# Softplus for two thirds of batch 0, masks ahead of the first sum, and a new order of instructions in a recurrence-and-mixer kernel

## The chip, the cores and the metric

The kernel runs on one core of a Trainium2 chip. Its engines work side by side, each through its own list of instructions: TensorE (PE, with its weight loads as PEld) for matrix products, VectorE (DVE), ScalarE (ACT) and GpSimd (POOL) for work on elements, and SyncE (SP), which only issues transfers. DMA engines move data between memory and the core; here SP, ACT and POOL issue these transfers. The metric is the time of one execution on the device in microseconds (us); lower is better.

## The reference

A gated linear recurrence runs over 768 steps for 4 batches and 8 heads of width 48, and its output goes through a mixer of two two-layer networks, one across the tokens and one across the channels.

```python
f = 1.0 / (1.0 + np.exp(-f_logit))
for t in range(S):
    state = f[:, :, t, :, None] * state + np.einsum('bhd,bhe->bhde', k[:, :, t], v[:, :, t])
    y[:, :, t] = np.einsum('bhd,bhde->bhe', q[:, :, t], state)
...
h = np.maximum(xt @ w_tok1, 0.0) @ w_tok2
u = x + h.transpose(0, 2, 1)
h2 = np.maximum(u @ w_ch1, 0.0) @ w_ch2
return (u + h2).astype(np.float32)
```

The kernel works with the logarithm of the gates: -log f = log(1 + exp(-f_logit)), which is Softplus of -f_logit.

## The kernel before

**Stages.** The 768 steps of a batch are cut into six chunks of 128, taken in pairs P = 0, 1, 2; the two steps of a pair that share a row are folded by an addition. For each batch b and pair P the stages are these.

- `gates` (line 447) makes -log f in place in `f_sb` with two passes on ACT, Exp (line 450) and Ln (line 452).
- `sums_and_turns` (line 456) adds the two steps into `two` (line 460), makes running sums with a triangular matrix `tri` on PE (line 472, and the totals at line 479), takes `first` from them (line 492), and exponentials of the sums into `GG` on ACT (lines 495 and 512). It multiplies q and k by `GG` into `qk` (line 516), and turns `qk` around into `qT` and `kT` (lines 541 and 543, later batches by a transfer).
- `attention` (line 556) makes scores from `kT` and `qT` (line 574), masks them into `AmT` (lines 612 to 617; for some of batch 0, ACT copies and POOL multiplies), updates the state from k and v (lines 592 and 626), copies it to `state_bd` (line 637) and forms the output of the pair (lines 650 and 658), which lands in `x_nat` and `x_bf`.
- `mixer` (line 697) runs the two networks over a batch: lines 702 and 718 across tokens, 759 to turn the result, 777 and 796 across channels. Line 802 adds the last product to `x_nat`, and SP stores the rows (line 695). The very last block is cut in two pieces, 288 and 96 columns wide.

**Masks and constants.** POOL makes `tri_bf` from ones (line 393). From it DVE makes `tri`, `tri2`, `ident` and six pieces of `mask` in eleven small steps (lines 396 to 408). `steady` holds the ones that fill matmuls read.

**Loads.** f of pair P0 of batch 0 comes in two halves, one issued by SP and one by ACT (`load_half`, line 342). SP issues f of P1 and, once POOL has marked it, f of P2. POOL issues everything else in one line: k and q of P0, v of P0, then k, q, v of P1 and of P2, the weights, and the later batches.

**What sets the order.** All steps are first collected in a plan. Each gets engines it may run on, what it needs, and a modelled cost. `ORDER` is a list written out in the file: each number, divided by four, names a step, and the rest of the division says which of its engines takes it. `best` (line 171) walks the list, gives each step a start time by the model, chooses the PSUM bank, and emits all steps sorted by that start. `SLOTS` and `HELD` are modelled landing times of loads. Every engine thus runs a fixed sequence, and waits are the only thing decided on the chip.

**Fills.** Where the model sees PE idle by over 250 ns ahead of 25.5 us, `best` inserts fill matmuls (`idle`, line 835), whose results nobody reads.

## Time and profile before

| | |
|---|---|
| median of three runs | 168.1 us (167.59 to 172.11) |
| the profiled execution, whole time | 167.82 us |
| its span, first to last instruction | 166.1 us |
| granted clock of PE | 1.00 of full speed |
| transferred | 24.34 MB, 68183 packets |

In the profile, a row of the timeline gives the start in us, the duration in us (of the merged row, if several follow each other), the engine, the line of the kernel, the operation, what it writes and reads, and how many instructions are merged. In brackets stands how long the engine was idle before it, and what ended that; "issue" means that nothing the profile shows was waited for. Durations of PE rows are partly modelled. In the rows of the DMA view the last number is the time from the issue to the landing in us.

### The profile page before, as it was taken

The page shows a single profiled execution, that of the slowest core. Times are in us where ns is not written, and L with a number is a line of the kernel's source. Part 1 is how long each engine was busy: PE and PEld are TensorE (multiplying, and loading weights), DVE is VectorE, ACT ScalarE, POOL GpSimd, SP SyncE. Part 2 cuts the span into 40 slices and gives each one's busy share as a digit, 9 for nine tenths or more (in the row PEclk, how much of TensorE's full clock was granted, in tenths as well). Part 3 has the DMA queues.
Part 4 walks back from the last instruction along what each step waited for, and adds up shares of the span by engine and source line. Part 5 has one row for each costly group of instructions (what it writes and reads, how often), then busy time and mean ns, then how long its engine had stood idle before and what let it go on. Part 6 is the DMA issues. An engine that isn't in the chain of part 4 may idle for free.

```text
span 166.1 us, 5049 instructions
## 1 busy us (share of the span) xinstructions
PE 158.2 (95%) x2086; PEld 103.8 (62%) x2086; DVE 129.3 (78%) x286; ACT 107.4 (65%) x228; POOL 63.6 (38%) x87
## 2 busy tenths in 40 slices
PE   5899969999999999999999999999999999999991
PEld 4587856566657775665656666656667665656660
DVE  6469994789999999999969989997897366915331
ACT  3788985899899999797799598375622522141200
POOL 7977589915877640020346623212122021000000
PEclk9999999999999999999999999999999999999999
DMA  5999999999999999698194999478310014900452
GB/s 131 218 176 173 201 211 240 188 233 208 211 222 218 249 226 248 76 92 213 20 126 99 165 146 113 116 134 178 64 45 8 4 36 107 329 3 4 143 189 95
DMA packets 68183, 24.34 MB, mean 147 GB/s; under 512 B 60896, under 2 KB 67296, under 8 KB 68160
## 3 DMA queue, kind: packets, MB, share of 16 engines
q0 software_dynamic: 41856, 13.77, 69.6%
q1 hardware_dynamic: 25776, 10.06, 28.5%
q8 instruction: 16, 0.26, 0.7%
q10 hardware_dynamic: 528, 0.20, 0.5%
q14 instruction: 7, 0.06, 0.1%
HBM read 25.17 MB, written 4.72 MB: 180 GB/s over the span
## 4 chain that ended last, share of the span: by engine, by line
PE 60%; DVE 2%; ACT 0%; issue 0%
PE ps L796 24%; PE ps L777 21%; PE ps L718 4%; PE ps L702 3%; PE ps L574 2%; PE ps L658 2%; PE ps L650 1%; DVE AmT L617 1%; PE ps L592 1%; PE ps L474 1%; DVE x_nat L802 1%; PE ps L759 1%; PE ps L475 1%; ACT state_bd L431 0%; DVE two L445 0%; DVE state L634 0%
## 5 line engine op out<-in xcount | busy, mean ns | idle before, releaser
L796 PE MATMUL ps<-w_ch,zT 128*128 128x384 bf16 (+2 forms) x300 | 52.5, 320 | 0.0
L777 PE MATMUL ps<-uT,w_ch 128*128 128x384 bf16 x288 | 50.9, 326 | 0.0
L777 PEld LDWEIGHTS <-w_ch 128*128 128x128 bf16 x288 | 27.7, 98 | 18.1 <-issue 0.4
L796 PEld LDWEIGHTS <-zT 128*128 128x128 bf16 x300 | 27.9, 98 | 17.0
L440 ACT ACTIVATE zT<-ps 128x384 bf16<-128x384 f32 x52 | 23.6, 494 | 16.8 <-PE ps L777 16.6
L617 DVE TENSOR_TENSOR AmT<-ps,mask 128x512 bf16<-128x512 f32 x44 | 28.8, 681 | 0.4 <-PE ps L574 0.3
L442 DVE TENSOR_SCALAR zT<-ps 128x384 bf16<-128x384 f32 x44 | 22.3, 549 | 8.5 <-PE ps L777 8.4
L802 DVE TENSOR_TENSOR x_nat<-x_nat,ps 128x384 f32<-128x384 f32 (+2 forms) x25 | 13.2, 532 | 7.5 <-PE ps L796 7.3
L435 POOL CAST state_bd<-state 48x192 bf16<-48x192 f32 x15 | 5.4, 358 | 25.7 <-DVE state L634 11.4
L445 DVE TENSOR_TENSOR qk<-qk_sb,GG 128x768 bf16<-128x768 bf16 x24 | 13.4, 585 | 1.2 <-ACT GG L512 0.9
L431 ACT ACTIVATE x_bf<-ps 128x384 bf16<-128x384 f32 x17 | 8.1, 491 | 8.8 <-DVE AmT L617 5.2
L354 POOL DMA_DIRECT2D v_sb<-in_v_dram x12 | 10.7, 892 | 6.9 <-DMA w_ch<-in_moe_w_ch_dram 4.9
L512 ACT ACTIVATE GG<-first 128x384 bf16<-128x384 f32 x24 | 11.7, 523 | 1.9 <-DVE first L492 1.8
L734 DVE TENSOR_TENSOR x_nat<-x_nat,ps 128x384 f32<-128x384 f32 x21 | 10.6, 547 | 2.8 <-PE ps L718 2.7
L435 POOL COPY qT<-qJ 128x1024 bf16<-128x1024 bf16 x5 | 5.7, 1148 | 16.9 <-DMA qJ<-qk 13.1
L495 ACT ACTIVATE GG<-ps 128x384 bf16<-128x384 f32 x24 | 11.3, 487 | 1.4 <-PE ps L475 0.8
L431 ACT ACTIVATE u_bf<-x_nat 128x384 bf16<-128x384 f32 x12 | 5.8, 517 | 9.7 <-issue 6.1
L354 POOL DMA_DIRECT2D qk_sb<-in_k_dram x12 | 10.9, 906 | 1.6 <-POOLq L855 0.8
L450 ACT ACTIVATE f_sb<-f_sb 128x768 f32<-128x768 f32 x12 | 10.1, 842 | 1.8 <-DMA f_sb<-in_f_logit_dram 1.8
L354 POOL DMA_DIRECT2D qk_sb<-in_q_dram x12 | 10.7, 894 | 0.8 <-DMA qk_sb<-in_q_dram 0.5
L837 PE MATMUL ps<-steady 128*128 128x256 bf16 x54 | 9.1, 330 | 1.7 <-DVE ones L372 1.7
L702 PE MATMUL ps<-x_bf,w_tok 128*128 128x384 bf16 x48 | 10.5, 327 | 0.0
(81 smaller groups left out, 230.2 us busy)
## 6 DMA issues: line engine op xcount, KB each, us to landing
out_dram<-x_nat SPq DMA_DIRECT2D x23, 192.0 KB, 2.2
f_sb<-in_f_logit_dram POOLq DMA_DIRECT2D x9, 384.0 KB, 8.8
qk_sb<-in_k_dram POOLq DMA_DIRECT2D x12, 192.0 KB, 8.7
qk_sb<-in_q_dram POOLq DMA_DIRECT2D x12, 192.0 KB, 8.6
v_sb<-in_v_dram POOLq DMA_DIRECT2D x12, 192.0 KB, 8.9
w_ch<-in_moe_w_ch_dram POOLq DMA_DIRECT2D x2, 576.0 KB, 13.5
w_ch<-in_moe_w_ch_dram POOLq DMA_DIRECT2D x1, 1152.0 KB, 11.8
f_sb<-in_f_logit_dram SPq DMA_DIRECT2D x2, 384.0 KB, 4.2
```

Source lines behind the costliest of these rows:

```text
L354: lambda eng=eng, into=held(dst[i], P), of=runs(src, b, P): eng.dma_start(out=into, in_=of),
L431: nc.scalar.activation(out_, in_, AF.Copy, bias=0.0, scale=1.0)
L440: nc.scalar.activation(out_, in_, AF.Relu, bias=0.0, scale=1.0)
L442: nc.vector.tensor_scalar(out_, in_, 0.0, None, ALU.max)
L445: (nc.vector if op.engine == DVE else nc.gpsimd).tensor_tensor(out_, a, b_, what)
L495: add(ACT, r, lambda n=n: nc.scalar.activation(GG[i][:, 1, n], sview(), AF.Exp, bias=0.0, scale=2.0 * n - 1.0), make=[("G", i, 1, n)], ban ...
L512: add(ACT, r, lambda n=n: nc.scalar.activation(GG[i][:, 0, n], first[i], AF.Exp, bias=0.0, scale=2.0 * n - 1.0), need=[("first", i)], make ...
L617: add(DVE, r, lambda into=into, made=made, m4=m4: nc.vector.tensor_tensor(into, made(), m4, ALU.mult), need=masks, make=[("AmT", i, js, pa ...
L702: add(PE, rank("tok1", rt), lambda rt=rt, kt=kt, pm=pm: nc.tensor.matmul(banks[pm.at][:, 0:DM], lhsT=w_tok1[:, kt, rt * 128:(rt + 1) * 128 ...
L777: nc.tensor.matmul(banks[pm.at][:, 0:384], lhsT=w[:, kt, c0:c0 + 128], rhs=uT[:, th, :, kt, :], start=(kt == 0), stop=(kt == 2))
L796: nc.tensor.matmul(banks[pm.at][:, 0:n1 - n0], lhsT=zT[:, kt, tt * 128:(tt + 1) * 128], rhs=w_ch2[:, kt, n0:n1], start=(kt == 0), stop=(kt ...
L802: add(DVE, rank("ch2", tt), lambda un=un, pm=pm, n=n1 - n0: nc.vector.tensor_tensor(un, un, banks[pm.at][:, 0:n], ALU.add), make=[("x_nat" ...
```

## The change

- **Softplus.** For P0 and P1 of batch 0 (`SOFT = (0, 1)`, "four chunks"), `gates` issues one Softplus pass instead of Exp and Ln. ACT therefore loads the table "softplus" first, and a second table with Exp and Ln after both passes; all exponentials of batch 0 need that second table.
- **Masks ahead.** The first addition into `two` now needs all masks, `ident` and `tri2`, so DVE runs these eleven steps before it.
- **Loads.** `LOADS` puts v of P1 behind k and q of P2 on POOL.
- **Fills.** A rest of over 80 ns (before: 250) is filled, and the number of fill matmuls is counted in single ones. `steady` is one column, read with a broadcast, and is set before `tri_bf`.
- **The last block.** The 96-wide piece must run behind the 288-wide piece.
- **Model constants.** `SLOTS`, `HELD` and some costs are changed; these act only through start times, bank choices and numbers of fills.
- **A new `ORDER`**, for all steps. Read out by engine, it says among other things: SP issues f of P1 first and then its half of f of P0 (before: the other way round). On POOL, k of pair P0 of batch 1 moves behind the masked products of all three pairs of batch 0 (before: behind that of P0 alone). P0's copy into `qT` goes from ACT to DVE, the first two copies of the state (line 637) from DVE to ACT, and `x_nat` of the second chunk from ACT to DVE. The last pieces of the program are a 384-wide block and then the 96-wide piece (before: a 384-wide block).

```diff
+SOFT = (0, 1)
+LOADS = (("v", 0), ("kq", 1), ("kq", 2), ("v", 1), ("v", 2))
...
-            if e == PE and free[PE] < until and t - free[PE] > 250:
-                n = int((t - free[PE] - 1000) / 430) if not free[PE] else int((t - free[PE] - 40) / 218)
+            if e == PE and free[PE] < until and t - free[PE] > 80:
+                n = int((t - free[PE] - 400) / 200) if not free[PE] else int((t - free[PE] + 30) / 109)
...
-    steady = st([128, 512], BF16, "steady")
+    steady = st([128, 1], BF16, "steady")
...
+    nc.vector.memset(steady, 1.0)
     nc.vector.memset(tri_bf, 1.0)
-    nc.vector.memset(steady, 1.0)
...
-    once(ACT, lambda: nc.scalar.preload_act_table_set("natural_log_exp_and_others"), ["table"], 1280)
+    once(ACT, lambda: nc.scalar.preload_act_table_set("softplus" if SOFT else "natural_log_exp_and_others"), ["table"], 1280)
...
-    load("v", 0, 0)
-    load("kqv", 0, 1)
-    load("kqv", 0, 2)
+    for what, P in LOADS:
+        load(what, 0, P)
...
+        if b == 0 and P in SOFT:
+            add(ACT, r, lambda: nc.scalar.activation(fb, fb, AF.Softplus, bias=0.0, scale=-1.0), make=[key, ("soft", P)], kind=el,
+                need=["table"] + ([("fb", P)] if P < 1 else []))
+            return
...
-        op = add((DVE, POOL) if b == 0 else DVE, r, None, need=[key], make=[("two", i)], kind=("el", DM, False, 1.2))
+        op = add((DVE, POOL) if b == 0 else DVE, r, None, need=[key] + (masks + ["ident", "tri2"] if b + P == 0 else []), make=[("two", i)], kind=("el", DM, False, 1.2))
...
+                    if b == B - 1:
+                        if n0:
+                            plan.ops[-1].before.update(closing)
+                        else:
+                            closing.append(plan.ops[-1])
...
+            if b == 0 and P == len(SOFT):
+                once(ACT, lambda: nc.scalar.preload_act_table_set("natural_log_exp_and_others"), ["tables"], 1280 if SOFT else 10,
+                     ["table"] + [("soft", p) for p in SOFT])
...
-        for _ in range(2 * n):
-            nc.tensor.matmul(banks[NBANK - 1][:, 0:256], lhsT=steady[:, 0:128], rhs=steady[:, 0:256], start=True, stop=True)
+        for _ in range(n):
+            nc.tensor.matmul(banks[NBANK - 1][:, 0:256], lhsT=steady.broadcast_to((128, 128)), rhs=steady.broadcast_to((128, 256)), start=True, stop=True)
```

26 lines of the change are left out of this document (13 added, 13 removed), and 110 rows, old and new, of the table ORDER.

## The prediction, made before the run

> **What bounds the kernel now.** I read the page first (busy time and the chain of waits), then the windows of the first 32 us, then the timeline of the start, then single rows of the DMA view.
>
> ```profile
> span 166.1 us, 5049 instructions
> PE 158.2 (95%) x2086; PEld 103.8 (62%) x2086; DVE 129.3 (78%) x286; ACT 107.4 (65%) x228; POOL 63.6 (38%) x87
> PE 60%; DVE 2%; ACT 0%; issue 0%
> ```
>
> The chain of waits lies on PE for 60% of the span: all of the last 100 us. Nothing in the diff takes real matmuls away, so that stretch can only begin earlier; its end moves with its start. What can be won lies ahead of it and in the store behind it.
>
> ```profile
> 12.00:14.00 2.00, 2.00 (x45) 1.70 (x40) 1.76 (x5) 1.62 (x2) 1.12 (x3) 1.00 2.02 171
> 22.00:24.00 2.00, 1.69 (x59) 1.19 (x57) 2.00 (x5) 1.77 (x6) 1.19 (x3) 1.00 1.16 209
> 28.00:30.00 2.00, 1.75 (x12) 0.93 (x11) 0.56 (x1) 0.65 (x2) 2.00 (x3) 1.00 1.95 180
> 62.80 0.33 PE L650 MATMUL ps<-state_bd,qT 128*128 128x96 bf16 x4 [0.41 <-ACT state_bd L431]
> ```
>
> In the windows the columns are PE, PEld, DVE, ACT, POOL, clock, DMA. The first two rows are the first and last of six from 12 to 24 us, in which DVE is busy 11.66 of 12 us: batch 0's attention is bound by DVE, and PE passes the time with fill matmuls. At 28 to 30 us PE is idle 0.25 us, at 62.80 it waits 0.41 us. The granted clock is 1.00 throughout.
>
> **The start.** From the timeline and the DMA view:
>
> ```profile
> 0.82 0.47 SPq L345 DMA_DIRECT2D f_sb<-in_f_logit_dram  x1
> 1.32 1.28 ACT L389 ACT_TABLE_LOAD   x1 [1.32 <-PEq L855]
> 1.35 2.67 SPq L354 DMA_DIRECT2D f_sb<-in_f_logit_dram  x2
> 3.30 0.30 POOL L393 TENSOR_SCALAR_AFFINE_SELECT tri_bf<-tri_bf 128x128 bf16<-128x128 bf16 x1
> 4.37 0.84 ACT L450 ACTIVATE f_sb<-f_sb 128x768 f32<-128x768 f32 x1 [1.77 <-DMA f_sb<-in_f_logit_dram]
> 5.25 0.84 ACT L452 ACTIVATE f_sb<-f_sb 128x768 f32<-128x768 f32 x1
> 6.12 0.56 DVE L445 TENSOR_TENSOR two<-f_sb 128x384 f32<-128x384 f32 x1 [2.42 <-ACT f_sb L452]
> 6.60 0.57 DVE L396 CAST tri<-tri_bf 128x128 f32<-128x128 bf16 x1
> 7.41 0.91 PE L472 MATMUL ps<-two,tri 128*128 128x384 f32 x2 [0.55 <-DVE ident L401]
> 8.95 0.94 ACT L512 ACTIVATE GG<-first 128x384 bf16<-128x384 f32 x2 [1.25 <-DVE first L492]
> 11.15 0.19 DVE L408 COPY mask<-tri 64x64 bf16<-64x64 bf16 x1
> 15.13 0.22 DVE L404 COPY mask<-tri 64x128 bf16<-64x128 bf16 x1
> f_sb<-in_f_logit_dram ACTq DMA_DIRECT2D x1, 192.0 KB, 3.5
> f_sb<-in_f_logit_dram SPq DMA_DIRECT2D x1, 192.0 KB, 3.2
> f_sb<-in_f_logit_dram SPq DMA_DIRECT2D x1, 384.0 KB, 4.2
> ```
>
> Before, chunk P0 goes: f landed 4.3, Exp, Ln, the add into `two`, four mask steps, first sum at 7.41, first exponential at 8.95. The diff drops the Ln (0.84 us) and lets the mask steps run while DVE waits for ACT. They are eleven rows from 6.60 to 15.13, 2.68 us in sum, and may start at 3.60 when `tri_bf` is made; the smaller `steady` memset shortens DVE's queue ahead of that, but `tri_bf` comes later anyway. So they end by 6.3 at the worst.
>
> But two things run against it. First, the new order has SP issue the whole f of P1 (384 KB) ahead of its half of f of P0. Before, the last of these three transfers landed at 1.35 + 4.2 = 5.55. With the same bytes in the same queues, whichever is last lands there; now it is P0's half. Its bounds are 0.53 later than now (0.82 + 0.53 + 3.2 = 4.55) and 5.55; I take 5.5, the row with all the bytes ahead. The page DMA: Bandwidth & Descriptors of the Trainium skill (Queues, rings and completion order) says that each engine consumes a ring's descriptors in ring order; by it the early bound is out, and the sum stays; no row here shows the order within a ring by itself.
>
> Second, ACT must load another table between the two Softplus passes and the first exponential. Softplus itself has no row; the same shape as Exp or Ln takes 0.84, and if it were two passes inside it would take 1.68. I take 0.84, as both rows of that shape agree. Then P0 5.55 to 6.39, P1 to 7.27, table load 1.28 (the only load in the trace) to 8.55, first exponential 8.6 against 8.95. The first sum starts at 6.39 + 0.56 + 0.04 = 7.0 and is done at 7.9, before the table: ACT, not the sum, is late next. Gain 0.35 to 0.4; with f early, P0 4.6 to 5.44, P1 to 6.28, table to 7.6, masks hold `two` to 6.86, first exponential at 7.85: gain 1.1. I take **-0.4**. The load's row was taken with nothing ahead of it on ACT; behind a running pass it may cost more, and I bound it at twice its row, 1.28 more (a rival below). The page ScalarE: Activation LUTs of the Trainium skill (What ACT_TABLE_LOAD costs) gives 1283 ns for the load, with which the row agrees, and about 1380 ns more for a drain at every switch; by it the sum would be 167.0.
>
> **The DVE stretch, 11 to 25 us.**
>
> ```profile
> 12.56 0.72 DVE L433 CAST state_bd<-ps 48x192 bf16<-48x192 f32 x2
> 13.16 1.02 ACT L431 ACTIVATE qT<-ps 128x1024 bf16<-128x1024 bf16 x1 [0.38 <-PE ps L539]
> 13.32 0.69 DVE L433 COPY kT<-ps 128x1024 bf16<-128x1024 bf16 x1
> ```
>
> Out of it go the last six of the mask rows, 11.15 to 15.13 (1.26 us in sum), and two casts of the state (0.72, to ACT). In come P0's qT copy from ACT (between 0.69, DVE's copy of that size, and ACT's 1.02) and one 384-wide copy out of PSUM (0.55, as in the last row quoted below). Net -0.74 to -0.41; I take **-0.4**, as ACT, with the casts, has P2's exponentials ready hardly earlier.
>
> v of P1 now comes behind k and q of P2:
>
> ```profile
> 13.82 0.74 POOL L361 DMA_DIRECT2D w_ch<-in_moe_w_ch_dram  x1 [0.44 <-DMA qk_sb<-in_q_dram]
> 14.95 0.93 POOL L354 DMA_DIRECT2D f_sb<-in_f_logit_dram  x1 [0.38 <-DMA v_sb<-in_v_dram]
> 17.46 0.43 PE L592 MATMUL ps<-v_sb,qk 64*64 64x48 bf16 x16
> ```
>
> POOL's queue waits for each of these landings in turn: q of P1 at 13.8, v at 14.95, so one transfer takes 1.13. Two later puts v at 17.2, and its first reader ran at 17.46. I cost it at nothing, under 0.2 us of cover; beyond that it delays the state of P1 one for one.
>
> **A stop of PE.**
>
> ```profile
> 23.27 0.42 PE L658 MATMUL ps<-v_sb,AmT 64*128 64x48 bf16 x19
> 24.85 0.34 PE L658 MATMUL ps<-v_sb,AmT 64*128 64x48 bf16 x13 [1.16 <-issue]
> 25.66 0.36 DVE L626 TENSOR_TENSOR ps<-ps,glast 128x192 f32<-128x192 f32 x1 [0.82 <-issue]
> q8 instruction: 1, 0.02, 3.0%
> ```
>
> One group of 32 matmuls, all with the same inputs, stops for 1.16 us after the 19th, and DVE behind it stands 0.82 us. No wait explains that; the DMA view of 22 to 24 us shows a packet of instructions (0.02 MB). I read it as PE running out of fetched instructions. The new order and the other number of fills put the block's edge elsewhere. Bounds: 0.82 gained if the edge falls where PE has fill, nothing if it falls on the path again. I take **-0.8**, since PE spends much of this stage in fills, where a stop costs nothing.
>
> **Fills** go in from 80 ns instead of 250. A fill that outlasts its rest delays PE by tens of ns; PE waits in this stage anyway: 0, and at most +0.5 if DVE should cease to be its cover.
>
> **Batch 1's loads.**
>
> ```profile
> 17.38 0.92 POOL L354 DMA_DIRECT2D qk_sb<-in_k_dram  x1
> 27.55 0.92 POOL L354 DMA_DIRECT2D f_sb<-in_f_logit_dram  x1
> f_sb<-in_f_logit_dram POOLq DMA_DIRECT2D x1, 384.0 KB, 11.9
> 40.95 0.83 ACT L450 ACTIVATE f_sb<-f_sb 128x768 f32<-128x768 f32 x1
> ```
>
> The k load of batch 1's P0 moves on POOL behind the last masked product, so all later loads come about one issue (0.92) later. f of P1 then lands at 27.55 + 0.92 + 11.9 = 40.4, still before its Exp at 40.95: nothing, with 0.6 us of cover left.
>
> **Later waits.** The two PE waits at 28 and 62.8 us are 0.66; a whole new order may close them and open others: **-0.4**, bounds -0.7 to +0.5.
>
> **The end.**
>
> ```profile
> 156.26 0.26 DVE L802 TENSOR_TENSOR x_nat<-x_nat,ps 128x96 f32<-128x96 f32 x1 [0.94 <-PE ps L796]
> 162.53 0.55 DVE L802 TENSOR_TENSOR x_nat<-x_nat,ps 128x384 f32<-128x384 f32 x1 [0.68 <-PE ps L796]
> out_dram<-x_nat SPq DMA_DIRECT2D x1, 48.0 KB, 1.8
> ```
>
> The last piece becomes the 96-wide one: 0.26 instead of 0.55. Its store queues on SP behind that of the 384-wide piece just ahead, which takes back some 0.1: **-0.2**.
>
> **Sum.** 0.4 + 0.4 + 0.8 + 0.4 + 0.2 = 2.2 us. The profiled execution took 167.82 (span 166.1 and 1.7 around it), near the median of 168.1 of three runs (167.59 to 172.11). 167.8 - 2.2 = **165.6**.
>
> **Rivals.**
> *Everything arrives* (164.2): f of P0 lands early after all (0.7 more), DVE gains its full 0.7 (0.3 more), both later waits go (0.3), the tail 0.1: 165.6 - 1.4. For it: the three transfers may share bandwidth as they please. Against: the bytes.
> *The table switch costs twice its row* (166.9): +1.28 on ACT between P1's Softplus and P0's exponentials, all of it on the path. For it: the one load in the trace can't show what a switch behind running work costs. Against: its 1.28 is all that any row has.
> *PE stops more often* (169.1, slower). Finer fills and smaller groups mean more PE instructions in the same microseconds, and each fetched block that comes late costs 1.16. The forecast counts none on the path; three give 165.6 + 3 x 1.16 = 169.1. From two on (167.9) nothing is gained; five would come to 171.4. For it: the stop in the trace, at a time when DMA is loaded. Against: just one in 18 us of such code.
> *The change not doing what it says*: one pass that costs two (Softplus at 1.68) adds 1.7 on ACT, 167.3; I count it with the dearer switch.
>
> **Chances.** Forecast 0.47, its own range 164.4 to 166.8; everything arrives 0.28; dearer switch or double pass 0.12; stops 0.13. The range that leaves out 2 in 10: 163.2 (1 us below the faster rival, for new waits closed that I can't see) to 169.1. Two per cent, about what a measurement of this kernel can tell from no change, is 164.7 and 171.5 against the median. Faster: the first rival and 0.07 of the forecast's lower edge, 0.35. Slower: the upper part of the stops, 0.05. Within: 0.60.
>
> **What would show it.** Right: two Softplus rows from 5.5, a table load ending near 8.6, no mask rows after 7, first sum at 7.0; DVE's last P2 mask product ending near 24 instead of 24.8; no `issue` wait above 0.5 in PE before 26 us; last DVE row 0.26 long. Wrong: Softplus starting at 4.6, an idle of over 1 us on ACT next to the second load, DVE idle between 11 and 24 us, or the solid PE stretch beginning later than now although the first sum came earlier.

## The result, and the profile after

The changed kernel takes 170.52 us in the median of four runs (170.38 to 173.04), the kernel before 168.16 (167.59 to 172.11). The ratio is 1.0149, with a 95% interval from 1.0115 to 1.0184: slower by one and a half per cent. Ratios, here and below, leave out runs that were slowed as a whole, while medians are over all runs. The profiled execution took 170.38 us, 2.56 more than the 167.82 of the profiled execution before, and its span is 168.7 us.

From the page of the changed kernel: its span, the busy time of each engine, and the chain of waits by engine.

```profile
span 168.7 us, 5104 instructions
PE 159.9 (95%) x2108; PEld 105.3 (62%) x2108; DVE 133.5 (79%) x293; ACT 102.6 (61%) x219; POOL 63.9 (38%) x88
PE 70%; DVE 14%; DMA 6%; ACT 5%; issue 2%; SPq 0%; DVEq 0%; ACTq 0%
```

A DMA share of 6% stands in the chain now; the page puts 3% of it down to `uT` and 3% to the load of f at the start. Before, the chain could be followed back over the last 62% of the span only, so its start cannot be compared. To see where the time went, each recorded matmul of PE was counted with the time it takes in a solid stretch (0.163 us for a 384-wide bf16 product, for instance), with the fills left out, and summed up to a given moment. This is the sum after less the sum before, in us; a minus means that the changed kernel is behind:

| up to | 8 | 12 | 16 | 24 | 32 | 60 | 105 | 110 | 160 us |
|---|---|---|---|---|---|---|---|---|---|
| after | +0.43 | +0.26 | -0.70 | -0.89 | -0.28 | -0.96 | -1.14 | -2.60 | -2.46 |

So the start is ahead by 0.26, batch 0 loses 0.54 from 12 to 32 us, the long stretch loses 0.86 from 32 to 105, and then 1.46 goes within 5 us. Each of these has its rows.

**The start**, from the timeline of the changed kernel:

```profile
0.81 0.47 SPq L356 DMA_DIRECT2D f_sb<-in_f_logit_dram  x1
1.34 0.67 SPq L347 DMA_DIRECT2D f_sb<-in_f_logit_dram  x1
5.76 1.58 ACT L452 ACTIVATE f_sb<-f_sb 128x768 f32<-128x768 f32 x2 [3.17 <-DMA f_sb<-in_f_logit_dram]
6.27 0.22 DVE L406 COPY mask<-tri 64x128 bf16<-64x128 bf16 x1
6.63 0.56 DVE L446 TENSOR_TENSOR two<-f_sb 128x384 f32<-128x384 f32 x1
7.25 1.65 PE L477 MATMUL ps<-two,tri 128*128 128x384 f32 x4 [1.61 <-DVE two L446]
7.35 1.28 ACT L839 ACT_TABLE_LOAD   x1
8.79 0.49 ACT L500 ACTIVATE GG<-ps 128x384 bf16<-128x384 f32 x1 [0.15 <-DVE first L497]
```

f of P0 lands late, as its bytes said; Softplus costs one pass; the second table load takes 1.28 and the next row stands 0.16 behind its end, where it waits for `first`. The first exponential comes 0.16 us earlier than before (8.95).

**Batch 0**, from the timeline of the changed kernel, and then of the kernel before:

```profile
12.31 1.23 DVE L434 COPY qT<-ps 128x1024 bf16<-128x1024 bf16 x1 [1.10 <-PE ps L544]
14.05 0.36 DVE L631 TENSOR_TENSOR ps<-ps,glast 128x192 f32<-128x192 f32 x1
14.44 0.66 ACT L432 ACTIVATE state_bd<-ps 48x192 bf16<-48x192 f32 x2 [0.70 <-DVE ps L631]
17.05 0.66 ACT L432 ACTIVATE state_bd<-ps 48x192 bf16<-48x192 f32 x2 [1.25 <-DVE ps L631]
17.73 0.87 ACT L500 ACTIVATE GG<-ps 128x384 bf16<-128x384 f32 x2
21.78 1.05 PE L544 MATMUL ps<-ident,qk 128*128 128x128 bf16 x16
23.81 2.67 DVE L622 TENSOR_TENSOR AmT<-ps,mask 128x512 bf16<-128x512 f32 x4
24.98 0.65 PE L707 MATMUL ps<-x_bf,w_tok 128*128 128x384 bf16 x3
28.17 1.46 PE L707 MATMUL ps<-x_bf,w_tok 128*128 128x384 bf16 x8
```

```profile
12.16 0.37 DVE L626 TENSOR_TENSOR ps<-ps,glast 128x192 f32<-128x192 f32 x1 [0.23 <-PE ps L592]
20.26 1.07 PE L539 MATMUL ps<-ident,qk 128*128 128x128 bf16 x16
27.27 1.46 PE L702 MATMUL ps<-x_bf,w_tok 128*128 128x384 bf16 x8
```

P2 is turned on PE at 21.78, 1.52 us later than before. DVE waits 1.10 us for PE ahead of the `qT` copy, and its first update of the state stands behind both copies, at 14.05 instead of 12.16. ACT's casts of the state wait for such updates: 0.70 us for the two that moved to ACT, and 1.25 us for the next two, which were on ACT before as well; P2's exponentials are queued behind these. From 12 to 24 us DVE is busy 10.67 of 12 us. The stop of 1.16 us is gone, and the last eight products across tokens come only 0.90 later.

**The long stretch**, one row of the windows view from 32 to 104 us, after and before (columns: length, then busy time and count on PE, PEld, DVE, ACT and POOL, granted clock, DMA share, GB/s):

```profile
32.00:104.00 72.00, 70.86 (x1002) 45.94 (x1000) 68.53 (x147) 62.25 (x135) 33.47 (x41) 1.00 1.33 166
```

```profile
32.00:104.00 72.00, 71.59 (x1001) 46.27 (x1001) 67.72 (x144) 63.63 (x138) 30.59 (x37) 1.00 1.32 169
```

PE stands still for 1.14 us of it, before for 0.41.

**The loss at 107 us**, from the timeline of the changed kernel, and then from its DMA view of 107.4 to 107.6 us and of 104.4 to 104.6 (queue, kind: packets, MB, share; and an issue with its time to landing):

```profile
104.51 1.30 SPq L753 DMA_TRANSPOSE uT<-u_bf  x1
105.86 1.26 SPq L513 DMA_DIRECT2D glast<-ends  x2
107.24 1.76 SPq L753 DMA_TRANSPOSE uT<-u_bf  x1
109.58 2.61 PE L782 MATMUL ps<-uT,w_ch 128*128 128x384 bf16 x15 [1.25 <-DMA uT<-u_bf]
```

```profile
q8 instruction: 1, 0.02, 29.8%
...
uT<-u_bf SPq DMA_TRANSPOSE x1, 5.0
```

Before, the transposes of `u_bf` into `uT` landed 3.2 us after their issue, and their reader never waited. Here the first one takes 5.0 (the last number of its row). The trace notes the arrival on each of the 16 DMA engines: fifteen of them were done from 107.81 to 107.97, the sixteenth at 109.53. From 107.51 to 108.46 one packet of 16 KB was moved that holds no data but instructions; the trace does not say on which engine.

**The end**, from the timeline of the changed kernel:

```profile
156.37 8.64 PE L801 MATMUL ps<-w_ch,zT 128*128 128x288 bf16 x64
...
161.88 4.31 SPq L700 DMA_DIRECT2D out_dram<-x_nat  x7
163.31 2.06 DVE L812 TENSOR_TENSOR x_nat<-x_nat,ps 128x384 f32<-128x384 f32 x4 [1.46 <-PE ps L801]
```

PE ends at 165.01, DVE's last add at 165.37, SP's last issue at 166.19, 0.82 later. Before, PE ended at 162.50, and the other two were 163.08 and 163.44, 0.36 apart.

### The profile page after: what moved, and what is told of

The parts are those of the page before. It is cut to its first block, busy times and chain, and to the rows that moved or that the text cites. A ratio compares the mean times of both kernels' runs of the same rounds, so it can differ in the third digit from the quotient of the medians.

```text
span 168.7 us, 5104 instructions
## 1 busy us (share of the span) xinstructions
PE 159.9 (95%) x2108; PEld 105.3 (62%) x2108; DVE 133.5 (79%) x293; ACT 102.6 (61%) x219; POOL 63.9 (38%) x88
## 4 chain that ended last, share of the span: by engine, by line
PE 70%; DVE 14%; DMA 6%; ACT 5%; issue 2%; SPq 0%; DVEq 0%; ACTq 0%
PE ps L782 22%; PE ps L801 20%; PE ps L850 4%; PE ps L707 3%; PE ps L579 3%; DVE AmT L622 3%; PE ps L663 3%; DMA uT<-u_bf 3%; PE ps L723 3%; DMA f_sb<-in_f_logit_dram 3%; DVE zT L443 2%; PE ps L655 2%; PE ps L544 2%; PE ps L597 2%; PE ps L484 2%
## 5 line engine op out<-in xcount | busy, mean ns | idle before, releaser
L782 PE MATMUL ps<-uT,w_ch 128*128 128x384 bf16 x288 | 50.0, 326 | 1.7 <-DMA uT<-u_bf 1.2
L801 PE MATMUL ps<-w_ch,zT 128*128 128x384 bf16 (+2 forms) x300 | 51.3, 320 | 0.0
L441 ACT ACTIVATE zT<-ps 128x384 bf16<-128x384 f32 x50 | 22.7, 491 | 20.9 <-PE ps L782 19.8
L443 DVE TENSOR_SCALAR zT<-ps 128x384 bf16<-128x384 f32 x46 | 23.4, 552 | 6.0 <-PE ps L782 6.0
L850 PE MATMUL ps<-steady 128*128 128x256 bf16 x76 | 12.2, 307 | 1.0 <-DVE steady L370 1.0
L432 ACT ACTIVATE x_bf<-ps 128x384 bf16<-128x384 f32 x15 | 7.0, 485 | 9.3 <-PE ps L663 5.1
L707 PE MATMUL ps<-x_bf,w_tok 128*128 128x384 bf16 x48 | 9.8, 327 | 0.0
L850 PEld LDWEIGHTS <-steady 128*128 128x128 bf16 x76 | 7.8, 111 | 3.0 <-DVE steady L370 1.0
L356 POOL DMA_DIRECT2D f_sb<-in_f_logit_dram x9 | 8.2, 906 | 2.3 <-issue 1.0
```

What stands on the lines that cost most here:

```text
L356: lambda eng=eng, into=held(dst[i], P), of=runs(src, b, P): eng.dma_start(out=into, in_=of),
L441: nc.scalar.activation(out_, in_, AF.Relu, bias=0.0, scale=1.0)
L443: nc.vector.tensor_scalar(out_, in_, 0.0, None, ALU.max)
L707: add(PE, rank("tok1", rt), lambda rt=rt, kt=kt, pm=pm: nc.tensor.matmul(banks[pm.at][:, 0:DM], lhsT=w_tok1[:, kt, rt * 128:(rt + 1) * 128 ...
L782: nc.tensor.matmul(banks[pm.at][:, 0:384], lhsT=w[:, kt, c0:c0 + 128], rhs=uT[:, th, :, kt, :], start=(kt == 0), stop=(kt == 2))
L801: nc.tensor.matmul(banks[pm.at][:, 0:n1 - n0], lhsT=zT[:, kt, tt * 128:(tt + 1) * 128], rhs=w_ch2[:, kt, n0:n1], start=(kt == 0), stop=(kt ...
```

## The experiments

Each kernel has a name, given with its time. Those named e1 to e4 ran on one chip, b1, e5, e6 and e8 on another, and b2, b3, e9 and e10 together on the first again; each group shares runs of the kernel before. Times are compared across groups by the ratio to that kernel. Where a theory speaks of P0's f, of masks or of fills, the names are those of the sections above. In `ORDER` a step's number is the entry divided by four.

### The transfer between the two transposes

```diff
-    3368, 2820, 2796, 2809, 3236, 3240, 3244, 3248, 3252, 2196, 2172, 3500, 2824, 3356, 2828, 3260, 3272, 2176,
+    3368, 2820, 2796, 2809, 3236, 3240, 3244, 3248, 3252, 2196, 2172, 3500, 2824, 2828, 3356, 3260, 3272, 2176,
```

> The changed kernel with one DMA issue moved: on SP, batch 3's glast row transfer for P1 (256 pieces of 16 bytes, not needed until after 125 us) is issued behind the second uT transpose of batch 2 instead of between the two. Theory (the transfer put between the transposes delays the landing of the first one from 3.2 to 5.0 us): PE's wait of 1.25 us at 109.58 goes, the time falls by 1.0 to 1.4 us against the changed kernel, to about 169.2. Rival (the transposes are late only because the u_bf casts ahead of them are about 2 us later in the new order): the first transpose still lands 5 us after its issue, the wait stays, and the time moves by less than 0.3 us.

Measured (e1_glast_after): 170.61 us in the median of ten runs, ratio to the kernel before 1.0128 (1.0080 to 1.0177). The wait is 1.10 us instead of 1.25, and the transpose still lands 4.9 us after its issue. The packet of instructions started at 107.17. The theory of the queue's order falls. The numbers are the rival's, but its reason doesn't reach: casts that come later move the issue, they don't lengthen the way from the issue to the landing. A third cause was needed, and the packet of instructions, just where the transpose ends, was the candidate.

### f of P0 first

```diff
-    0, 4, 24, 28, 32, 12, 16, 20, 8, 188, 192, 196, 36, 48, 52, 40, 44, 76, 60, 56, 72, 64, 68, 208, 212, 356,
+    0, 4, 24, 28, 32, 12, 16, 8, 20, 188, 192, 196, 36, 48, 52, 40, 44, 76, 60, 56, 72, 64, 68, 208, 212, 356,
```

> The changed kernel with SP's half of f of P0 issued ahead of the whole f of P1, as before the change. Theory (transfers in one queue land in the order of issue, so P0's half now comes behind 384 KB): first Softplus near 4.6 instead of 5.76, P1's Softplus near 5.5, table load done near 7.7, first sum held to about 7.1 by the mask steps, first exponential near 8.0 instead of 8.79; if all of that reached the end the time would fall by 0.8, and I expect about 0.4, as DVE is the next bound. Rival (the transfers share bandwidth and the order of issue does not matter): first Softplus stays at 5.6 to 5.8 and the time moves by less than 0.2.

Measured (e2_f_first): 171.45 us in the median of four runs, ratio 1.0131 (1.0016 to 1.0245). From its timeline:

```profile
4.30 0.84 ACT L452 ACTIVATE f_sb<-f_sb 128x768 f32<-128x768 f32 x1 [1.69 <-DMA f_sb<-in_f_logit_dram]
5.46 0.84 ACT L452 ACTIVATE f_sb<-f_sb 128x768 f32<-128x768 f32 x1 [0.32 <-DMA f_sb<-in_f_logit_dram]
6.53 1.03 DVE L446 TENSOR_TENSOR two<-f_sb 128x384 f32<-128x384 f32 x2
8.68 0.49 ACT L500 ACTIVATE GG<-ps 128x384 bf16<-128x384 f32 x1 [1.08 <-DVE first L497]
```

The order of issue decides what lands first: 4.30 against 5.76, with the same bytes. But the masks hold DVE until 6.5, so the first exponential gains 0.11 us, not 0.8. PE is mostly 0.1 to 0.3 us ahead of the changed kernel until 100 us, and all of that goes into the wait at 108 us, which is 1.39 long here.

### The copies back on their old engines

```diff
-    220, 228, 236, 224, 240, 360, 364, 216, 368, 244, 80, 84, 248, 88, 260, 264, 384, 388, 232, 376, 372, 200,
-    252, 296, 256, 300, 92, 96, 268, 272, 204, 304, 308, 280, 380, 504, 392, 396, 292, 508, 312, 316, 276, 288,
+    220, 228, 236, 224, 240, 360, 364, 216, 368, 244, 80, 84, 248, 88, 260, 265, 384, 388, 232, 376, 372, 200,
+    252, 296, 256, 300, 92, 96, 268, 272, 204, 305, 309, 280, 380, 504, 392, 396, 292, 508, 312, 316, 276, 288,
```

> The changed kernel with three copies of batch 0's P0 put back on the engines they had before: the qT copy on ACT, the two casts of the state on DVE, in the same places of the order. Theory (what PE lost between 12 and 24 us came from the new split of work between DVE and ACT): kT's copy comes 1.2 us earlier, P1's qk steps too, PE regains 0.3 to 0.6 us by 24 us, time down by 0.3 to 0.6. Rival (DVE has as much work in that stretch either way, and P2's products end where they ended): time within 0.2.

Measured (e3_dve_back): 172.45 us, ratio 1.0207 (1.0103 to 1.0310): worse by some 2 us. From its timeline:

```profile
12.27 1.02 ACT L432 ACTIVATE qT<-ps 128x1024 bf16<-128x1024 bf16 x1 [1.83 <-PE ps L544]
13.19 0.93 ACT L517 ACTIVATE GG<-first 128x384 bf16<-128x384 f32 x2
```

ACT now waits 1.83 us for PE's turned block, and P1's exponentials, which in the changed kernel belong to a row that begins at 9.96, stand behind it. kT's copy did come 0.74 earlier, to no use. Both theories miss. Put back alone, the old split makes the new order worse, since the order around it is made for the new one; what the new split costs the change is not shown by this. At 24 us PE's sum of work is 2.23 us behind the kernel before, against 0.89 in the changed kernel.

### The old rule for the fills

```diff
-            if e == PE and free[PE] < until and t - free[PE] > 80:
-                n = int((t - free[PE] - 400) / 200) if not free[PE] else int((t - free[PE] + 30) / 109)
+            if e == PE and free[PE] < until and t - free[PE] > 250:
+                n = int((t - free[PE] - 1000) / 215) if not free[PE] else int((t - free[PE] - 40) / 109)
```

> The changed kernel with the old rule for fills: only rests of over 250 ns are filled, with the old counts (the operand stays the broadcast single column). Theory (fills cover rests and cost tens of ns each): time within 0.3 us, useful PE work between 12 and 24 us unchanged within 0.2. Rival (fills that outlast their rest delay the real matmuls behind them; 22 more of them): PE's useful work comes 0.5 to 0.9 us earlier by 24 us and the time falls by as much. A fall of the granted clock would show as a slower start instead.

Measured (e4_fills_old): 168.22, 172.74, 173.09 and 173.92 us, too far apart for a verdict. The profiled one is that of 173.09:

```profile
1.00 4.66 PE L850 MATMUL ps<-steady 128*128 128x256 bf16 x21 [1.00 <-DVE steady L370]
7.46 2.93 PE L477 MATMUL ps<-two,tri 128*128 128x384 f32 x4 [1.80 <-DVE two L446]
```

Four sums take 2.93 us where they took 1.65. Four fills fewer stand ahead of them, and PE rests 1.80 us instead of 1.61, but the rest is not where the rate went: all 21 fills start 0.21 us apart, whereas in the changed kernel the first 16 do and the others, from 4.5 us on, start 0.11 apart. PE had never been at full rate here, and reached it at 16.7 us only. That says nothing on the rule. It led to the next kernel.

### The old rule, and no rest ahead of the first sum

```diff
-            if e == PE and free[PE] < until and t - free[PE] > 80:
-                n = int((t - free[PE] - 400) / 200) if not free[PE] else int((t - free[PE] + 30) / 109)
+            if e == PE and free[PE] < until and t - free[PE] > 250:
+                n = int((t - free[PE] - 400) / 200) + 11 if not free[PE] else int((t - free[PE] - 40) / 109)
```

> The changed kernel with the old rule for the fills inside batch 0 (only rests of over 250 ns) and with 11 fills more ahead of the first sum, so that PE does not stand still for 1.6 us before it. In the run with the old rule alone the first sum came behind a rest of 1.80 us and PE ran its matmuls at half their rate from 7.5 to 15 us (2.93 us for four 384-wide f32 sums against 1.65). Theory (that half rate is set by the rest of PE ahead of the first sum): the four sums take 1.65 again, and useful PE work at 28 us is within 0.3 us of the changed kernel, as the finer fills cost nothing. Rival (the finer fills delay real matmuls by 0.5 to 0.9 us in all): PE's useful work is that much earlier by 28 us.

Measured (e8_old_fills_warm): 170.07 us in nine runs from 169.77 to 170.27, ratio 1.0105 (1.0065 to 1.0144). The sums run at full rate:

```profile
1.00 6.65 PE L850 MATMUL ps<-steady 128*128 128x256 bf16 x36 [1.00 <-DVE steady L370]
7.49 1.46 PE L477 MATMUL ps<-two,tri 128*128 128x384 f32 x4
```

At 28 us PE stands at -0.49 against -0.81 in the changed kernel, though its first sum came 0.24 later. That lies between the two expectations: the finer fills do cost, but about 0.3 us. At 110 us half of it is left (-2.44 against -2.60), since the wait for the transpose is 1.5 us here.

### The same fills in half as many instructions

```diff
-        for _ in range(n):
-            nc.tensor.matmul(banks[NBANK - 1][:, 0:256], lhsT=steady.broadcast_to((128, 128)), rhs=steady.broadcast_to((128, 256)), start=True, stop=True)
+        for w in [512] * (n // 2) + [256] * (n % 2):
+            nc.tensor.matmul(banks[NBANK - 1][:, 0:w], lhsT=steady.broadcast_to((128, 128)), rhs=steady.broadcast_to((128, w)), start=True, stop=True)
```

> The changed kernel with its fills of the same total width in half as many instructions: 512 columns instead of 256, so that PE has 35 matmuls fewer in the first 28 us and nothing else is different. Theory (the loss of 1.4 us at 105 to 110 us is a collision: a 16 KB packet of instructions, at 107.51 in the changed kernel, holds one DMA engine while the first uT transpose of batch 2 has its last pieces there; where the packet falls depends on how many PE instructions went before): the packet falls at another place, by up to 2.4 us, the transpose lands about 3.2 us after its issue instead of 5.0, PE's wait of 1.25 us goes, the time falls by 1.1 to 1.4 us to about 169.2. Rival (transposes issued there are slow for another reason, such as the order of the queue): the landing stays near 5 us and the time within 0.3 us.

Measured (e5_wide_fills): 169.29 us in nine runs from 168.78 to 171.06, ratio 0.9994 (0.9948 to 1.0039), against 1.0149 for the changed kernel. The profiled execution took 171.06, as its sums ran at half rate (PE had rested 1.92 us ahead of them), but its transposes are what matters: the packet came at 110.19, 3.56 us behind the issue, the first transpose landed after 3.2, and PE's sum of work does not change between 105 and 110 us. The forecast of 169.2 held; of the eight shorter runs that give it there is no trace.

### An early start

```diff
-    0, 4, 24, 28, 32, 12, 16, 20, 8, 188, 192, 196, 36, 48, 52, 40, 44, 76, 60, 56, 72, 64, 68, 208, 212, 356,
-    220, 228, 236, 224, 240, 360, 364, 216, 368, 244, 80, 84, 248, 88, 260, 264, 384, 388, 232, 376, 372, 200,
+    0, 4, 24, 28, 32, 12, 16, 8, 20, 188, 192, 196, 36, 48, 52, 40, 44, 76, 60, 208, 56, 212, 356, 220, 72, 228,
+    236, 224, 240, 360, 364, 216, 64, 68, 368, 244, 80, 84, 248, 88, 260, 264, 384, 388, 232, 376, 372, 200,
...
-        op = add((DVE, POOL) if b == 0 else DVE, r, None, need=[key] + (masks + ["ident", "tri2"] if b + P == 0 else []), make=[("two", i)], kind=("el", DM, False, 1.2))
+        op = add((DVE, POOL) if b == 0 else DVE, r, None, need=[key], make=[("two", i)], kind=("el", DM, False, 1.2))
```

> The changed kernel with SP's half of f of P0 issued ahead of f of P1, and with four of the mask steps put behind the first sum again (those that make the two masks of P1 and P2 halves; the sum's own triangle stays ahead). Theory (with the early f alone the first sum was held by the mask steps until 7.1, so the first exponential won 0.1 us only): first Softplus near 4.3, first sum near 5.9, the table load ends at 7.6 and is the bound, first exponential near 7.7 instead of 8.79. What of these 1.1 us is left at 60 us shows how far DVE behind it is the bound: I expect PE's useful work there to be 0.6 to 0.9 us earlier than in the changed kernel, and the end by 0.5 to 1.0 earlier unless the transpose at 105 us takes it back. Rival (batch 0 is bound by DVE alone): below 0.3 us at 60 us.

Measured (e6_early_start): 169.55 us in nine runs, ratio 1.0057 (1.0015 to 1.0100). From its timeline:

```profile
6.27 1.28 ACT L839 ACT_TABLE_LOAD   x1
7.57 0.49 ACT L500 ACTIVATE GG<-ps 128x384 bf16<-128x384 f32 x1
103.71 1.30 SPq L753 DMA_TRANSPOSE uT<-u_bf  x1
108.78 4.40 PE L782 MATMUL ps<-uT,w_ch 128*128 128x384 bf16 x26 [1.51 <-DMA uT<-u_bf]
```

The table load is the bound, as expected, and the first exponential comes 1.22 us earlier than in the changed kernel. At 60 us PE is 1.04 ahead of it (+0.08 against -0.96): what the start gains is kept, so batch 0 is not bound by DVE alone. Then the transpose, again 5.0 us under way, costs 1.63 by the sum, where it cost the changed kernel 1.46.

### Softplus alone, on the kernel before

```diff
-    0, 4, 8, 20, 12, 16, 24, 28, 32, 188, 192, 196, 200, 212, 36, 48, 40, 216, 52, 360, 224, 240, 244, 44, 252,
+    0, 4, 8, 20, 12, 16, 24, 28, 32, 188, 192, 196, 200, 36, 48, 40, 52, 212, 216, 360, 224, 240, 244, 44, 252,
...
-    once(ACT, lambda: nc.scalar.preload_act_table_set("natural_log_exp_and_others"), ["table"], 1280)
+    once(ACT, lambda: nc.scalar.preload_act_table_set("softplus"), ["table"], 1280)
...
-        add(ACT, r, lambda: nc.scalar.activation(fb, fb, AF.Exp, bias=0.0, scale=-1.0), make=[key], kind=el,
+        add(ACT, r, lambda: nc.scalar.activation(fb, fb, AF.Softplus if b == 0 and P < 2 else AF.Exp, bias=0.0, scale=-1.0), make=[key], kind=el,
...
-        add(ACT, r, lambda: nc.scalar.activation(fb, fb, AF.Ln, bias=1.0, scale=1.0), make=[key], kind=el)
+        add(ACT, r, lambda: (nc.scalar.activation(fb, fb, AF.Ln, bias=1.0, scale=1.0) if b or P > 1 else nc.scalar.preload_act_table_set("natural_log_exp_and_others") if P else None), make=[key], kind=el if b or P > 1 else ("fix", 1280 * P, 1280 * P))
```

> The kernel before with one part of the change alone: Softplus in place of Exp and Ln for P0 and P1 of batch 0, the second table load behind the two passes, and the four small steps that the first sum needs (triangle and identity) ahead of the first add on DVE. Order, loads and fills' rule as before the change. Theory (Softplus and its table load are sound; the change lost time in its order and in the collision): Softplus at 4.4 and 5.5, load done at 7.6, first sum near 5.9, first exponential 7.7 instead of 8.95, time 0.5 to 1.0 us below the kernel before. Rival 1 (the switch of tables costs twice its row): first exponential near 8.9, no gain. Rival 2 (DVE is the bound from 11 us on whatever the start): less than 0.2 us.

Measured (b1_softplus): 168.30 us (167.25 to 168.35), ratio 0.9897 (0.9807 to 0.9987). From its timeline:

```profile
6.33 1.28 ACT L452 ACT_TABLE_LOAD   x1
7.63 0.94 ACT L512 ACTIVATE GG<-first 128x384 bf16<-128x384 f32 x2
24.06 0.32 PE L658 MATMUL ps<-v_sb,AmT 64*128 64x48 bf16 x11 [1.11 <-issue]
```

```profile
24.00:28.00 4.00, 3.94 (x77) 2.91 (x78) 1.70 (x5) 1.60 (x4) 4.00 (x6) 0.60 1.25 250
```

The load is over at 7.61 and the exponential follows 0.02 later: the switch has no second cost, and rival 1 falls. The stop of PE is there as before, 0.79 us earlier. The profiled execution lost its gain from 24 to 28 us, where the granted clock was 0.60 (the last row, of the windows view): by the trace's record it was 0.50 from 24.83 to 28.25, 0.77 us behind the end of the stop; the interval of the ratio leaves a gain between 0.1 and 1.9%, so rival 2 is unlikely but its size is not settled by these three runs.

### The same with half as many fills

On the kernel of the last run:

```diff
-        for _ in range(2 * n):
-            nc.tensor.matmul(banks[NBANK - 1][:, 0:256], lhsT=steady[:, 0:128], rhs=steady[:, 0:256], start=True, stop=True)
+        for _ in range(n):
+            nc.tensor.matmul(banks[NBANK - 1][:, 0:512], lhsT=steady[:, 0:128], rhs=steady[:, 0:512], start=True, stop=True)
```

> The kernel of the run b1_softplus (the kernel before, with Softplus and the first sum's steps ahead) with its fills of the same width in half as many instructions (512 columns each), 28 matmuls fewer in the first 21 us. In b1_softplus the stop of PE with no wait behind it was still there, 1.11 us ahead of 24.06. Theory (the stop is PE out of instructions: a 16 KB packet is asked for at a certain count of PE's instructions, and where the next 1 to 2 us hold 64-row matmuls of 17 ns each, PE gets through its stock before the packet is there): the packet comes later by the 28 matmuls, 0.5 to 1.5 us, the stop shrinks below 0.4 us or falls among 384-wide matmuls, and the time is 1.0 to 1.8 us below the kernel before. Rival (the stop belongs to the products at that place): still 1.1 us, time as b1_softplus, 0.5 to 0.9 below the kernel before.

Measured (b2_softplus_wide): 167.55 us in twelve runs, ratio 0.9915 (0.9883 to 0.9946), 0.9% below the kernel before by this ratio. The traces show less: its profiled execution took 167.90, the kernel before 167.82, and PE's sums of work are within 0.2 us from 100 us on; the runs of the kernel before in this group that the ratio uses go from 167.50 to 169.94. The stop, from its timeline:

```profile
23.09 0.57 PE L658 MATMUL ps<-v_sb,AmT 64*128 64x48 bf16 x32
24.12 0.40 PE L592 MATMUL ps<-v_sb,qk 64*64 64x48 bf16 x14 [0.46 <-DVE AmT L617]
24.92 0.21 PE L592 MATMUL ps<-v_sb,qk 64*64 64x48 bf16 x2 [0.40 <-issue]
```

It has moved to another group of products and shrunk to 0.40, as forecast.

### One rest of the kernel before in finer fills

```diff
-        for _ in range(2 * n):
-            nc.tensor.matmul(banks[NBANK - 1][:, 0:256], lhsT=steady[:, 0:128], rhs=steady[:, 0:256], start=True, stop=True)
+        for w in [256] * 4 + [128] * 44 if n == 13 else [256] * (2 * n):
+            nc.tensor.matmul(banks[NBANK - 1][:, 0:w], lhsT=steady[:, 0:128], rhs=steady[:, 0:w], start=True, stop=True)
```

> The kernel before with nothing but its first fill cut finer: 44 matmuls of 128 columns and 4 of 256 in place of 26 of 256, 22 matmuls more in the same rest. Theory (the packets of instructions come by PE's count of instructions): the packet that fell at 106.96 falls 2 to 4 us earlier, in 103 to 105 us, where the first uT transpose of batch 2 (issued at 102.5, landed at 105.7) is on its way; if it falls on the transpose's last pieces the landing goes from 3.2 to about 5 us. Its reader starts at 106.95, so only 1.25 us of a late landing are hidden and the loss is at most 0.5 us here. The stop at 23.7 us moves too, by 22 matmuls, and the time may fall by up to 1.1 with it. Rival (packets come by time or by another engine's count): packet within 0.5 us of where it was, landing 3.2, stop where it was, time within 0.2.

Measured (b3_packet_moved): 169.86 us in twelve runs, ratio 1.0034 (0.9985 to 1.0083). The packet did not come where I wanted it: it fell at 109.76, 4.1 us behind the issue of the first transpose. The profiled execution is 3.1 us late there by PE's sum of work, so the packet moved by about 0.3 us against the work and not by 2 to 4. For this packet the rival held: it does not come by PE's count. The landing stayed at 3.2, so this kernel does not test the collision. For the stop the theory held:

```profile
25.68 0.30 PE L650 MATMUL ps<-state_bd,qT 128*128 128x96 bf16 x3 [1.33 <-issue]
```

The stop is among other products now. Counted from the first fill on, PE stops behind its matmul number 351 here; it does behind number 351 in the kernel before and in b1_softplus, and behind number 350 in b2_softplus_wide, e8_old_fills_warm and e10_early_wide_old, whatever product that is.

### The early start with half as many fills

On the kernel of "An early start":

```diff
-        for _ in range(n):
-            nc.tensor.matmul(banks[NBANK - 1][:, 0:256], lhsT=steady.broadcast_to((128, 128)), rhs=steady.broadcast_to((128, 256)), start=True, stop=True)
+        for w in [512] * (n // 2) + [256] * (n % 2):
+            nc.tensor.matmul(banks[NBANK - 1][:, 0:w], lhsT=steady.broadcast_to((128, 128)), rhs=steady.broadcast_to((128, w)), start=True, stop=True)
```

> The kernel of the run e6_early_start (f of P0 first, four mask steps behind the first sum) with fills of 512 columns in half as many instructions. e6_early_start was level with the kernel before at 100 us and then lost 1.8 us to the late uT transpose, with the packet at 106.71. Theory: without the collision it ends level with the kernel before, 1.6 to 1.8 us below e6_early_start, at 167.4 to 168.0. Rival (the wait at 107 us comes back by another cause): within 0.4 us of e6_early_start.

Measured (e9_early_wide): 167.73 us in twelve runs from 167.57 to 168.22, ratio 0.9943 (0.9916 to 0.9969). From its timeline:

```profile
103.27 1.30 SPq L753 DMA_TRANSPOSE uT<-u_bf  x1
105.96 2.21 SPq L753 DMA_TRANSPOSE uT<-u_bf  x1
106.93 6.34 PE L782 MATMUL ps<-uT,w_ch 128*128 128x384 bf16 x38
```

The reader runs without a wait, and PE's sum of work stays at 0.00 against the kernel before from 105 to 110 us, where e6_early_start went from -0.16 to -1.79. The number expected, 167.4 to 168.0, is met.

### And with the old rule

On the kernel just told; the first rest keeps the new count:

```diff
-            if e == PE and free[PE] < until and t - free[PE] > 80:
-                n = int((t - free[PE] - 400) / 200) if not free[PE] else int((t - free[PE] + 30) / 109)
+            if e == PE and free[PE] < until and t - free[PE] > 250:
+                n = int((t - free[PE] - 400) / 200) if not free[PE] else int((t - free[PE] - 40) / 109)
```

> As e9_early_wide, with the old rule of filling only rests of over 250 ns. Theory (in the run e8_old_fills_warm the old rule was worth 0.3 us by 28 us): 0.2 to 0.4 us below e9_early_wide if the packets of instructions fall as well as there, so about 0.3 to 0.5 us below the kernel before. Rival (the finer fills cost nothing, and the 0.3 was the warmer start): level with e9_early_wide within 0.15.

Measured (e10_early_wide_old): 167.35 us in twelve runs from 167.12 to 167.72, ratio 0.9937 (0.9905 to 0.9969). That is 0.38 us below e9_early_wide by the medians of the same chip, as expected, and 0.6% below the kernel before by the ratio, or 0.3% by the two profiled executions (167.32 and 167.82). Part of the gain is given back at matmul 350:

```profile
25.00 0.30 PE L663 MATMUL ps<-v_sb,AmT 64*128 64x48 bf16 x11 [0.37 <-issue]
```

### The runs side by side

For each kernel: the issue of the first `uT` transpose of batch 2, the start of the packet of instructions nearest behind it, the time between the two, the transpose's landing after its issue, and PE's wait (all us, from the traces).

| kernel | issue | packet | behind | landing | wait |
|---|---|---|---|---|---|
| before | 102.47 | 106.96 | 4.49 | 3.24 | 0 |
| after | 104.51 | 107.51 | 3.00 | 5.02 | 1.25 |
| e1_glast_after | 104.45 | 107.17 | 2.72 | 4.88 | 1.10 |
| e2_f_first | 104.45 | 107.41 | 2.96 | 5.00 | 1.39 |
| e6_early_start | 103.71 | 106.71 | 3.00 | 5.02 | 1.51 |
| e8_old_fills_warm | 104.49 | 107.27 | 2.78 | 4.95 | 1.54 |
| e9_early_wide | 103.27 | 106.49 | 3.22 | 3.22 | 0 |
| e5_wide_fills | 106.63 | 110.19 | 3.56 | 3.23 | 0 |
| e10_early_wide_old | 102.89 | 106.59 | 3.70 | 3.24 | 0 |
| e4_fills_old | 109.00 | 111.70 | 2.70 | 3.22 | 0 |

In five kernels the packet falls 2.7 to 3.0 us behind the issue, in the last half microsecond of the transpose, and all five land 1.7 us late. From 3.2 on none does. The one exception is e4_fills_old, at 2.70 and on time. In b1, b2 and b3 the packet falls over 4 us behind and in e3_dve_back ahead of the issue, and these land after 3.2 too. The window is narrow: e9_early_wide escaped by 0.2 us.

All transposes into `uT` in all 14 traces say it more broadly. There are 56. The 38 on whose way no packet starts land 3.2 to 3.3 us after their issue. Of the 18 on whose way one does, 11 land after 3.5 to 5.0: the five above, all five with the packet 0.36 to 1.00 us behind the issue, and the second transpose of e8_old_fills_warm, which stands behind a late one. The other seven land on time: six with the packet 0 to 0.30 us behind, and e4_fills_old's. So no transpose was late without a packet on its way; that the packet keeps a DMA engine from it is my reading, as the trace does not tell the packet's engine.

What the fills did to this packet is not what the theory said. From the changed kernel to e5_wide_fills there are 35 fills fewer, and when the packet starts 31 matmuls fewer have started (1552 and 1521); from e6_early_start to e9_early_wide 33 fills and 33 matmuls fewer (1551 and 1518). The packet thus stands at the same place of the work and not at the same count of PE; ACT has started 206 recorded instructions in all four. The fills changed the packet's distance to the transpose by 0.56 and 0.22 us, and that this was enough was luck.

And PE's work against the kernel before, as in the first table:

| up to | 12 | 24 | 32 | 60 | 105 | 110 | 160 us |
|---|---|---|---|---|---|---|---|
| after | +0.26 | -0.89 | -0.28 | -0.96 | -1.14 | -2.60 | -2.46 |
| e8_old_fills_warm | +0.20 | -0.31 | -0.06 | -0.57 | -0.81 | -2.44 | -2.46 |
| e6_early_start | +0.90 | +0.01 | +0.43 | +0.08 | -0.16 | -1.79 | -1.65 |
| e9_early_wide | +0.90 | +0.01 | +0.43 | +0.08 | 0.00 | 0.00 | +0.14 |
| e10_early_wide_old | +0.90 | +0.40 | +0.92 | +0.57 | +0.36 | +0.49 | +0.46 |

## Why the prediction was wrong, point by point

The forecast was 165.6 with a range to 169.1; the time is 170.5. The step that failed is the one the whole sum stood on: that the last 100 us "can only begin earlier" and that its "end moves with its start". It began later: by the sum of work PE is 0.28 us behind at 32 us and 0.96 at 60, although the first sum came earlier, which the list of signs had as one of being wrong. And its end did not move with its start: in that stretch the new order lost 0.86 us in small waits up to 105 us and 1.46 us on a transpose. Of the 4.8 us by which the forecast missed, some 1.9 lie in the first 32 us (1.6 forecast as a gain, 0.28 lost), 2.7 in the stretch behind it (2.3 lost, 0.4 counted on as a gain) and 0.2 at the end. I had costed what the diff does in the first 32 us and at the end, and given the remaining 70% of the kernel, whose order is new as well, a term of -0.4.

**The start, -0.4: 0.16 to the first exponential.** What the list of signs asked for nearly came: f at 5.76 (5.55 taken), Softplus at 0.84 a pass, a load that ends at 8.63 (8.55 taken). The step that was mis-sized is "ACT, not the sum, is late next": the first sum came at 7.25 instead of 7.0, because Softplus of P0 ended at 6.60 and not at 6.39 (the masks ended at 6.49, not "by 6.3 at the worst", but did not hold it), and `first`, 0.56 us on DVE behind the sum, was ready at 8.75, 0.12 behind the load's end. The sum for an early f leaves this step out: 6.86, the sum's 0.9 and the 0.56 give 8.4 and not 7.85, and e2_f_first shows 8.68. The early and the late bound for f are both shown now: 4.30 with P0's half ahead, 5.76 with it behind, with the same bytes. So here the order of issue decides. This agrees with the Trainium skill (DMA: Bandwidth & Descriptors, Queues, rings and completion order), by which each engine consumes a ring's descriptors in ring order.

**The table switch.** The rival's 1.28 us more was not there. In the changed kernel the next ACT row stands 0.16 behind the load and waits for DVE, in b1_softplus 0.02, in e6_early_start 0.02. By the drain that the Trainium skill gives for each switch (ScalarE: Activation LUTs, What ACT_TABLE_LOAD costs) the exponential would have come about 1.4 later; these rows don't show it, and the measurement decides.

**The DVE stretch, -0.4: a loss.** Masks and casts left DVE, as said, but its last P2 product of masks ends at 26.48, not near 24. The step that failed here is that DVE's work sets the time. In the new order it does not: DVE is idle 1.33 us between 12 and 24 us, before 0.34, and "DVE idle between 11 and 24 us" was on the list of signs of being wrong. It waits 1.10 us for PE ahead of the qT copy, which then takes 1.23 us, outside my bounds of 0.69 and 1.02; the state's update comes 1.9 us later behind it, and ACT waits for the updates, with P2's exponentials queued behind. What each of these waits costs wasn't tried: putting the copies back in the new order makes a longer wait of the same kind (1.83 us, e3_dve_back).

**The stop of PE, -0.8: right in its cause.** The stop is bound to the count of PE's instructions, shown by b3_packet_moved and by the number 350 or 351 in six kernels. In the changed kernel number 351 is one of three 384-wide products at 24.98, each 0.16 long, and nothing stops; that it falls there, and not among fills as I had it, was not worked out, so the term is partly luck. The traces also say when PE stops. Take the second 16 KB packet of instructions in each span, which starts between 21.5 and 27.2 us. The six kernels that stop go on 1.23 to 1.45 us behind its end (23.46 and 24.85 in the kernel before); the other eight reach matmul 351 by themselves 1.35 to 2.27 us behind it. PE stops where it gets there sooner. The gain was spent in the same 8 us by P2's late start.

**Fills, 0 and at most +0.5: about 0.4.** e8_old_fills_warm against the changed kernel has 0.32 by 28 us, e10_early_wide_old against e9_early_wide 0.38 in the medians. The bound was right, the value taken wasn't: in this stage PE's own delays are kept, up to 105 us in the sums of work.

**v of P1, batch 1's loads: 0, and 0.** No row of PE waits for v between 9 and 30 us, and f of P1 of batch 1 is there when ACT reads it at 41.62.

**Later waits, -0.4: +0.86.** Between 32 and 105 us the waits that the profile names went from 0.4 (state_bd) to 1.0 (uT, two_lo and qT, of 0.4, 0.4 and 0.2). These were not taken apart by runs; e9_early_wide and e10_early_wide_old still have them, and lose 0.43 and 0.56 from 32 to 105 us.

**Not on the list: the transpose, +1.46.** Its cause is shown as far as the 56 transposes go: none is late without a packet of instructions on its way, and where the packet falls at another place the wait is gone (e5_wide_fills, e9_early_wide, e10_early_wide_old). These edits touch the fills and the start, but they move other times as well; the one kernel made to bring packet and transpose together, b3_packet_moved, did not. I had the packets of instructions as a rival ("PE stops more often", 169.1), but only as a thing that PE waits for itself. That such a packet could also hold up a transfer was not among the mechanisms.

**The tail, -0.2: nothing.** From PE's end to the span's end it was 3.62 us and is 3.66. The last add got 0.3 us shorter, and its store waits longer on SP behind the one ahead: DVE's end to SP's last issue went from 0.36 to 0.82, where I had put the give-back at 0.1.

**What stays open**: which of the order's moves delay P2 by 1.5 us in batch 0, and which open the waits at 33 us, at 58 us and after; which engine's instructions the packet at 107 us holds, and what sets its time; why e4_fills_old escaped with its packet at 2.70; and why in e1_glast_after and e8_old_fills_warm all 16 engines were late (109.18 to 109.44) and not one.

## What to carry to other kernels

A new order of instructions is a change to every stage it covers, also where the diff shows nothing else: give each stage a term, and look there for transfers whose reader stands right behind them, as the time between the landing and the reader can shrink in any reordering (1.2 us before; 0.6 in the changed kernel, had the transpose taken 3.2). Look at what moves beside the data: fills of the same width in half as many instructions ended a collision worth 1.8 us with a packet of instructions, but it escaped by 0.2 us, so the edit is no remedy to rely on. And a step that is moved to another engine takes its wait with it: ahead of the qT copy ACT stood 0.38 us, and now DVE stands 1.10, with all that is queued behind.

## What the hardware showed that I had not expected

- PE stops at a fixed number of its own matmuls, 350 or 351 (with as many weight loads), by 0.3 to 1.3 us, where it gets there less than 1.2 us behind the end of the second 16 KB packet of instructions in its span. In five kernels short products (17 ns each) had brought it there fast; in e8_old_fills_warm it stopped 0.28 us between a fill and a 384-wide product.
- When a 16 KB packet of instructions, 0.9 us long, started 2.7 to 3.0 us behind the issue of a transpose of 128x1152 elements, the transpose landed 1.7 to 1.8 us late in five kernels of six, in the changed kernel on one of the 16 engines alone. With the packet 0.36 to 1.00 us behind the issue it landed 0.2 to 0.9 us late.
- Full rate can come late and go again. In e4_fills_old it came at 16.7 us, in the changed kernel at 4.5. In e5_wide_fills it was there from 3.9 us; PE then rested 1.92 us, and from 7.35 to 10.77 the granted clock was 0.50 and four f32 sums took 2.85 us. Behind a rest of 1.61 us in the changed kernel they took 1.65. A stop of 1.11 us (b1_softplus) was followed by 3.41 us at 0.50 as well, one of 1.16 us in the kernel before was not. The Trainium skill (TensorE: Matmul & The Clock Gate, Part 1) puts the idle window for this at about 3.4 us; here shorter rests were enough.
